# Top-k attention into a cosine-gated MLP: small VectorE steps between MAX8, the P@V scale on GpSimd, the weight shift and weight loads moved

## The chip, the cores and the metric

The kernel runs on one core of a Trainium2 chip. The metric is the device time of one execution in microseconds. The abbreviations are those of the profile: PE is TensorE's matmul, PEld its weight load, DVE is VectorE, ACT is ScalarE, POOL is GpSimd, SP is SyncE, which here only issues DMAs. "L475" is line 475 of the kernel before.

## The reference

Everything is float32 in meaning; the two weight matrices arrive as 64-bit floats.

```python
# q, k, v: (8, 8, 576, 64); w_in: (512, 2048); w_out: (2048, 512)
scores = matmul(q, k.T) / sqrt(64)
kth = partition(scores, -32)[..., -32:-31]          # the 32nd largest of each row
scores = where(scores >= kth, scores, -1e9) - max
attn = exp(scores) / (sum(exp(scores)) + 1e-9)
x = matmul(attn, v)  -> (4608 tokens, 512)           # heads side by side
h = x @ w_in
out = (h * cos(h)) @ w_out                           # (4608, 512)
```

## The kernel before, in words

**Units and slots.** Attention is cut into 144 units of 128 tokens and two heads. A unit's scores are a tile of 128 x 2 x 576. The main loop has 145 slots. In slot i the code works on several units at once: it searches the top 32 of unit `u` = i, finishes the softmax of `w` = i - 1, sends `x` = i - 2 through DRAM to be transposed, and, in even slots only, multiplies the pair `z` = (i - 4, i - 3) with V. Slots 0 to 8 are `early_slot`, 9 to 140 are `slot`, 141 to 144 `last_slot`. The schedule is manual: each engine runs its instructions in the order in which the Python code emits them.

**Search (VectorE).** `fold_high` (L244) takes the larger of each two scores into `rest` (288 wide), and GpSimd makes the smaller ones in `low` by an integer sum and difference (`fold_sum` L262, `fold_low` L271). `topk_round` then runs MAX8 (L342) and MATCH_REPLACE8 (L345) on the two heads: three rounds with replacement and a fourth without on `rest`, then two on `low`. `low` and `rest` have one buffer each, so `fold_sum` of a unit waits for the last search on `low` of the unit before. Between two units' searches stand small steps: `merge_first` (L330) and `merge_second` (L335) find the 32nd value of `w`, `bounds` (L354, L359) makes its negative and the exponent's bias, and `reciprocal` (L385, L386) adds up the softmax sums of `x` and inverts them.

**Softmax (ScalarE).** `mask` (L366, L368) and `exponentials` (L376). `take_scores` (L233, L234) copies the scores of the next unit out of PSUM.

**The way of P to the matmul.** `send(x)`: GpSimd's `split` (L403, L405) writes the float words as 16-bit halves, with the reciprocal appended; SP writes them to DRAM (`write_halves`, L413), waits for the landing, and issues a transposing DMA (`transposes`, L419) into `pT`. Two slots later at most, PE's `values` (L456) multiplies with V into the PSUM tile `rim`, ACT's `take_values` (L463) copies the result of two units to `xT`, and `scale_values` (L475, on VectorE) multiplies `xT` by the transposed reciprocal.

**MLP.** Per block of 128 tokens: `ff1` (L521) on PE, `take_first` on ACT (L535, L537), then on GpSimd the range reduction `reduce_first` (L557) and `reduce_second` (L566), the sine on ACT (`sines`, L576), the product on GpSimd (`gate`, L583), `ff2` (L596) on PE, and the output (L606). `feed(n)` emits up to n of these matmul pieces at fixed places of a slot; how many is a matter of a credit counter and of counters of finished steps, all in Python, so the order is fixed when the program is built.

**Order of a slot before.** `reciprocal(x)`; `topk_first` (merges of `w`, folds of `u`, `bounds(w)`, round 0); `decode_second`; `send(x)`; `fold_low`; rounds 1 to 3; then `feed(1)`; from slot 28 on `values(z)` and then the scores of the next units (before slot 28 the scores come first); the ACT steps; `scale_values(z)`; weight loads and the loads of q, k, v; `gate(1)`; `feed`; the range reduction; `feed`. In the steady part GpSimd's order is: in even slots `fold_sum`, `split`, `fold_low`, `reduce_first`, `reduce_second`; in odd slots `fold_sum`, `split`, `fold_low`, `gate`.

**Weights.** 32 chunks are loaded as 64-bit words into a ring of seven buffers, shared with the MLP's `g` tiles (`load_weights`, L115), and turned into float32 by ACT (`decode_first`, L128), GpSimd and VectorE (`decode_second`, L138 and the shift L141) and GpSimd (`decode_third`, L151). This ends in slot 13.

Of the kernel before, what the change touches and what calls it, by code (L numbers as in the profile page):

```python
# [10 lines left out]
F32 = mybir.dt.float32  # L11
# [4 lines left out]
ALU = mybir.AluOpType  # L16

P = 128
TOPK = 32
# [11 lines left out]
def kernel(  # L31
# [9 lines left out]
    nc = tc.nc  # L41
    ctx.enter_context(tc.manual_schedule())
    B, H, D, S = qT.shape
    DM, DF = moe_w_in.shape
    NT = S // P
# [4 lines left out]
    HS = S // 2  # L50
# [7 lines left out]
    small = ctx.enter_context(tc.tile_pool(name="small", bufs=4))  # L58
# [25 lines left out]
    for i in range(DF // CW):  # L84
        w = consts.tile([P, NC, CW], F32, tag=f"w_in{i}", name=f"w_in{i}")
# [47 lines left out]
    def decode_second(n):  # L133

        for _ in range(min(n, len(wq["second"]))):
            st, w = wq["second"].popleft()
            wi, lo = w.bitcast(I32), st[:, :, 0]
            nc.gpsimd.tensor_scalar(  # L138
                out=lo, in0=lo.bitcast(U32), scalar1=2.0**-29, scalar2=1.0, op0=ALU.mult, op1=ALU.mult
            )  # L140
            nc.vector.tensor_scalar(  # L141
                out=wi, in0=wi, scalar1=3, scalar2=None, op0=ALU.logical_shift_left
            )
            wq["third"].append((st, w))
# [121 lines left out]
    def fold_low(u):  # L266

        if not u["folds"]:
            return
        low = u["low"].bitcast(I32)  # L270
        nc.gpsimd.tensor_tensor(  # L271
            out=low, in0=low, in1=u["rest"][:, :, HS:S].bitcast(I32), op=ALU.subtract
        )
# [15 lines left out]
    def topk_first(u, w):  # L289

        u["top"] = tops[u["n"] % len(tops)]
        merges = w and w["folds"]
        if merges:
            merge_first(w)
        if u["folds"]:
            if u["n"] > EARLY:
                fold_sum(u)
            fold_high(u)
        else:
            u["rest"] = work.tile([P, 2, S], F32, tag="rest", name="rest", bufs=1)  # L300
        if merges:
            merge_second(w)
        if w:
            bounds(w)
        if u["folds"] and u["n"] <= EARLY:
            fold_now(u)
        topk_round(u, 0)

    def topk_round(u, rnd):
        top, rest, lasts = u["top"], u["rest"], TOPK // 8 - 1  # L310
        end = TOPK - 1 - 8 * rnd
        at = top[:, :, end : end - 8 if rnd < lasts else None : -1, 0]
        if u["folds"]:
            search(at, rest[:, :, HS:S] if rnd == 0 else rest[:, :, 0:HS], rest[:, :, 0:HS], rnd < lasts)
        else:
            search(at, u["s"] if rnd == 0 else rest, rest, rnd < lasts)
        if rnd < lasts:
            return
        del u["rest"]
        if u["folds"]:  # L320
            low = u.pop("low")
            for k in range(TOPK // 16):
                search(top[:, :, 1 + 8 * k : 9 + 8 * k, 1], low, low, k < TOPK // 16 - 1)

# [10 lines left out]
            op=ALU.max,  # L337
        )

    def search(to, src, rest, more):  # L340
        for j in range(2):
            nc.vector.max(to[:, j], src[:, j])  # L342
        if more:
            for j in range(2):
                nc.vector.match_replace(rest[:, j], to[:, j], src[:, j], NEG)  # L345

    def bounds(u):

        top = u.pop("top").rearrange("p j r i -> p j (r i)")
        end = 2 * TOPK  # L350
        if not u["folds"]:
            nc.vector.tensor_copy(out=top[:, :, end - 1], in_=top[:, :, 0])
        u["less"] = top[:, :, end : end + 2]
        nc.vector.tensor_reduce(  # L354
            out=u["less"], in_=top[:, :, end - 2 : end].unsqueeze(3), axis=mybir.AxisListType.X,
            op=ALU.max, negate=True,
        )
        u["nd"] = small.tile([P, 2], F32, tag="nd", name="nd")
        nc.vector.tensor_reduce(  # L359
            out=u["nd"], in_=top[:, :, end - 1 : end + 1], axis=mybir.AxisListType.X, op=ALU.add  # L360
        )

    def mask(u):
# [15 lines left out]
            )  # L379


    def reciprocal(u):
        u["rden"] = small.tile([P, 2], F32, tag="rden", name="rden")
        den = small.tile([P, 2], F32, tag="den", name="den")
        nc.vector.tensor_reduce(out=den, in_=u.pop("den"), axis=mybir.AxisListType.X, op=ALU.add)  # L385
        nc.vector.reciprocal(u["rden"], den)  # L386

    def normalise(u):
        s, rden = u["s"], u.pop("rden")
# [81 lines left out]
    def scale_values(us):  # L471

        for u in us:
            to = block_of[u["tok"]]["xT"][:, u["hp"]]
            nc.vector.tensor_tensor(out=to, in0=to, in1=u.pop("pT")[:, 2 * NT + 1], op=ALU.mult)  # L475

    widths = [P] * (B * S // P)
    blocks, block_of = [], {}
# [100 lines left out]
    def gate(n):  # L579
        for _ in range(min(n, len(sined))):  # L580
            blk, g, x = sined.popleft()
            eng = nc.vector if ff["end"] else nc.gpsimd
            eng.tensor_tensor(out=g, in0=g, in1=x, op=ALU.mult)  # L583
            blk["gated"].append(ff["tick"])
# [98 lines left out]
    def early_slot(i, u, w):  # L683
        n = 3 if i < 6 else 2
        topk_first(u, w)
        if i == 0:
            decode_second(1)
        scores(units[i + 1])
        for load, b, hp in at_slot.get(i, []):
            load(b, hp)  # L690
        load_weights(n)
        if w:
            mask(w)
            exponentials(w)
        topk_round(u, 1)

        decode_second(n)
        if w:
            reciprocal(w)
        topk_round(u, 2)  # L700
        topk_round(u, 3)
        if w:
            normalise(w)
        take_banks()
        take_scores(units[i + 1])
        gate(1)
        decode_third()
        feed(2)
        reduce_first()
        reduce_second()  # L710
        if i != NP:
            decode_first(n - 1)
        if w:
            transposes_now(w)
        feed(1)
        decode_first(n - len(wq["second"]))
        if w:
            values([w])
            take_values([w])
        feed(2)  # L720
        sines(2)
# [5 lines left out]
        transposes(x)  # L727

    def slot(i, u, w, x, z):
        if x:  # L730
            reciprocal(x)
        if u:
            topk_first(u, w)
            decode_second(2)
        if x:
            send(x)
        if u:
            fold_low(u)
            topk_round(u, 1)
            topk_round(u, 2)  # L740
            topk_round(u, 3)
        made = scored.get(i, [])
        if z:
            take_banks()
        feed(1)

        ahead = i < EARLY + 5 * NP
        if z and not ahead:
            values(z)
        for m in made:  # L750
            scores(m)
        if z and ahead:
            values(z)


        late = len(made) > 0

        decoding = i < EARLY + 8
        if i % 2 and not decoding:
            sines(1)  # L760
        if w:
            mask(w)
        take_banks()
        if w and late:
            exponentials(w)
        if z and not ahead:
            take_values(z)
        take_scores(units[i + 1])
        if z and ahead:
            take_values(z)  # L770
        if z:
            scale_values(z)
        if w and not late:
            exponentials(w)
        load_weights(2)
        for load, b, hp in at_slot.get(i, []):
            load(b, hp)
        gate(1)
        feed(1 if len(made) == 2 else 2)
        take_banks()  # L780
        decode_third()
        decode_first(2)
        reduce_first()
        reduce_second()
        feed(1 if len(made) == 2 else 3)
        if decoding or i == LAST:
            sines(1)

    def last_slot(i, u, w, x, z):
        if x:  # L790
            reciprocal(x)
        if u:
            topk_first(u, w)
            fold_low(u)
            topk_round(u, 1)
        if not u:
            bounds(w)
        mask(w)
        exponentials(w)
        take_banks()  # L800
        sines(1)
        if z:
            values(z)
        if i + 1 < NU:
            scores(units[i + 1])
        if z:
            take_values(z)
            scale_values(z)
        if i + 1 < NU:
            take_scores(units[i + 1])  # L810
        if x:
            send(x)
        reciprocal(w)
        normalise(w)
        if u:
            topk_round(u, 2)
            topk_round(u, 3)
        gate(2)
        feed(2)
        transposes_now(w)  # L820
        take_banks()
        reduce_first()
        reduce_second()
        feed(1)
        values([w])
        take_values([w])
        feed(2)
# [71 lines left out]
```

## Time and profile before

| what | value |
|---|---|
| median of 3 runs | 1504.34 us (1501.29 to 1507.36) |
| the profiled execution | 1504.25 us |
| its span | 1502.3 us |
| PE, PEld busy | 1414.7, 1015.1 us |
| DVE, ACT, POOL busy | 1392.8, 1096.0, 1162.0 us |
| mean granted TensorE clock | 0.966 |
| slots 28 to 139 (starts of L330) | 312.4 to 1387.2 us |

The span is the time from the first to the last instruction that the profile holds; the execution is 1.95 us longer. Busy time is the union of the instructions' intervals; since matmuls are pipelined and their ends are modelled, busy PE is not the same as PE at its peak. Small shapes are written partitions x elements. The lines below `## 5` of the page give for each group the count, the busy time, the mean duration of one in ns, and the idle time of the engine just before them with what ended it.

### The profile page before, as it was taken

To read this page: it belongs to the slowest core of one execution; us is meant where nothing else is said; L and a number is where in the kernel's file an instruction comes from. 1 tells how busy PE (TensorE), PEld (TensorE's weight loads), DVE (VectorE), ACT (ScalarE), POOL (GpSimd) and SP (SyncE) were. 2 spreads that over 40 slices of the span, in tenths; PEclk is the share of its full clock that TensorE was granted. 3 is DMA by queue.
4 is the path that set the end of the run, shared out by engine and by line. 5 is a ranking of instruction groups with operands and counts; after the bars stand their busy time and mean duration, and the time that the engine had idled before them with its cause. 6 is when DMAs were issued, how large, how long until landed. Compare 5 with 4: busy or idle time off the path is not lost.

```text
span 1502.3 us, 30590 instructions
## 1 busy us (share of the span) xinstructions
PE 1414.7 (94%) x10360; PEld 1015.1 (68%) x10360; DVE 1392.8 (93%) x5209; ACT 1096.0 (73%) x1974; POOL 1162.0 (77%) x836
## 2 busy tenths in 40 slices
PE   4778599999999999999999999999999999999899
PEld 3566267776777667777767767677677776777675
DVE  7998899999999999999989999999999998999931
ACT  4665667777777777777777777777777786777551
POOL 4678877888888888888878888888888887888510
PEclk6689799999999999999999999999999999999999
DMA  8423475556655566556655566645765556555200
GB/s 276 147 97 107 139 200 150 164 148 186 168 161 146 148 194 181 163 148 180 177 164 146 144 176 179 173 138 168 196 173 143 147 163 162 164 149 148 78 8 14
DMA packets 405549, 229.54 MB, mean 153 GB/s; under 512 B 355088, under 2 KB 371728, under 8 KB 405392
## 3 DMA queue, kind: packets, MB, share of 16 engines
q1 hardware_dynamic: 399984, 217.93, 52.5%
q10 hardware_dynamic: 5408, 9.65, 1.7%
q8 instruction: 82, 1.34, 0.4%
q14 instruction: 75, 0.61, 0.1%
HBM read 45.09 MB, written 95.94 MB: 94 GB/s over the span
## 4 chain that ended last, share of the span: by engine, by line
DVE 63%; PE 22%; ACT 6%; DMA 5%; issue 2%; POOL 1%; SPq 1%; POOLq 0%; DVEq 0%; ACTq 0%
DVE top L342 28%; DVE rest L345 17%; PE mm L521 9%; PE o L596 8%; DVE low L345 6%; DVE rest L244 5%; PE rim L456 3%; DMA pT<-rows 3%; PE sc L223 2%; DVE xT L475 2%; ACT s L376 1%; DVE top L354 1%; DVE top L330 1%; DVE nd L359 1%; DMA v<-in_v_dram 1%
## 5 line engine op out<-in xcount | busy, mean ns | idle before, releaser
L521 PEld LDWEIGHTS mm<-xT,w_in 128*128 128x128 f32 x4608 | 539.0, 192 | 77.1 <-issue 65.3
L596 PE MATMUL o<-w_out,g 128*128 128x512 f32 x1152 | 541.8, 604 | 19.1 <-POOL w_out L151 15.9
L521 PE MATMUL mm<-xT,w_in 128*128 128x128 f32 x4608 | 544.4, 276 | 7.3 <-DVE xT L475 3.9
L342 DVE MAX8 top<-rest 128x8 f32<-128x288 f32 x1148 | 469.9, 451 | 0.0
L345 DVE MATCH_REPLACE8 rest<-top,rest 128x288 f32<-128x288 f32 (+1 forms) x860 | 376.9, 445 | 0.0
L262 POOL TENSOR_TENSOR low<-s 128x576 int32<-128x576 int32 x133 | 192.6, 1448 | 198.5 <-DVE den L385 119.3
L596 PEld LDWEIGHTS o<-w_out,g 128*128 128x128 f32 x1152 | 203.8, 192 | 207.6 <-issue 181.4
L403 POOL COPY halves<-s 128x2304 uint16<-128x2304 uint16 x132 | 278.1, 2107 | 0.2
L376 ACT ACTIVATE s<-s,nd 128x576 f32<-128x576 f32 x288 | 220.6, 768 | 14.0 <-ACT ob L606 13.2
L342 DVE MAX8 top<-low 128x8 f32<-128x288 f32 x568 | 229.2, 446 | 0.0
L368 ACT ACTIVATE s<-s,top 128x576 f32<-128x576 f32 x288 | 206.1, 766 | 0.0
L535 ACT ACTIVATE g<-mm 128x512 f32<-128x512 f32 x144 | 85.9, 596 | 159.7 <-PE mm L521 155.1
L271 POOL TENSOR_TENSOR low<-low,rest 128x576 int32<-128x576 int32 x133 | 188.3, 1416 | 0.6 <-DVE top L335 0.5
L456 PE MATMUL rim<-pT,v 128*64 128x128 f32 (+1 forms) x2560 | 164.2, 273 | 19.4 <-DMA pT<-rows 10.5
L456 PEld LDWEIGHTS rim<-pT,v 128*64 128x64 f32 x2560 | 134.8, 141 | 70.0 <-ACT nd L366 22.0
L223 PE MATMUL sc<-k,q 64*128 64x448 f32 (+1 forms) x640 | 157.1, 592 | 10.7 <-DMA k<-in_k_dram 10.2
L566 POOL TENSOR_TENSOR x<-g,x 128x1024 f32<-128x1024 f32 x68 | 160.7, 2363 | 5.7
L583 POOL TENSOR_TENSOR g<-g,x 128x1024 f32<-128x1024 f32 x68 | 160.7, 2363 | 3.7 <-ACT x L576 3.7
L233 ACT COPY s<-sc 128x896 f32<-128x896 f32 x144 | 130.4, 906 | 4.2 <-PE sc L223 4.2
L345 DVE MATCH_REPLACE8 low<-top,low 128x288 f32<-128x288 f32 x284 | 123.6, 443 | 0.0
L463 ACT COPY xT<-rim 128x256 f32<-128x256 f32 (+1 forms) x78 | 27.8, 357 | 128.0 <-PE rim L223 104.2
L244 DVE TENSOR_TENSOR rest<-sc,s 128x576 f32<-128x576 f32 x142 | 106.3, 748 | 8.2 <-ACT s L234 8.2
(59 smaller groups left out, 1387.4 us busy)
## 6 DMA issues: line engine op xcount, KB each, us to landing
rows<-halves SPq DMA_DIRECT2D x132, 640.0 KB, 3.1
out_dram<-ob ACTq DMA_DIRECT2D x36, 256.0 KB, 3.0
q<-in_q_dram SPq DMA_DIRECT2D x31, 288.0 KB, 3.4
st<-in_moe_w_in_dram SPq DMA_DIRECT2D x16, 512.0 KB, 5.6
v<-in_v_dram SPq DMA_DIRECT2D x32, 256.0 KB, 3.1
st<-in_moe_w_out_dram SPq DMA_DIRECT2D x16, 512.0 KB, 3.9
k<-in_k_dram SPq DMA_DIRECT2D x31, 144.0 KB, 3.6
k<-in_k_dram SPq DMA_DIRECT2D x32, 128.0 KB, 3.5
```

Source lines behind the costliest of these rows:

```text
L223: nc.tensor.matmul(to[r0 : r0 + rows, j, 0 : k1 - k0], st["q"][d, q0 : q0 + rows], st["k"][d, k0:k1], start=True, stop=True,)
L244: nc.vector.tensor_tensor(out=u["rest"][:, :, HS:S], in0=sc[:, :, 0:HS], in1=s[:, :, HS:S], op=ALU.max)
L262: nc.gpsimd.tensor_tensor(out=u["low"].bitcast(I32), in0=s[:, :, 0:HS], in1=s[:, :, HS:S], op=ALU.add)
L271: nc.gpsimd.tensor_tensor(out=low, in0=low, in1=u["rest"][:, :, HS:S].bitcast(I32), op=ALU.subtract)
L342: nc.vector.max(to[:, j], src[:, j])
L345: nc.vector.match_replace(rest[:, j], to[:, j], src[:, j], NEG)
L368: nc.scalar.activation(out=s[:, j], in_=s[:, j], func=AF.Prelu, bias=less[:, j, 1:2], scale=1.0, alpha=FAR)
L376: nc.scalar.activation(out=s[:, j], in_=s[:, j], func=AF.Exp, bias=nd[:, j : j + 1], scale=SCALE, accum_out=den[:, j, 0:1],)
L403: nc.gpsimd.tensor_copy(out=halves[:, :, 0 : 2 * S], in_=s.rearrange("p (k h) -> p h k", h=2))
L456: nc.tensor.matmul(o[d, to], lhsT, rhs, start=c == 0, stop=c == NT)
L521: nc.tensor.matmul(mm[:, at : at + w], w_in[f // FC][:, c, (f % FC) * P : (f % FC + 1) * P], blk["xT"][:, c], start=c == 0, stop=c == NC - 1,)
L596: nc.tensor.matmul(o, g[:, at : at + P], w_out[f], start=f == 0, stop=f == NF - 1)
```

## The change

- `search` takes a list `between`: after the MAX8 of each of the two heads one small step is put. In round 0 these are the two steps of `bounds(w)`, now `bounds` and `distances`; in the last search of a unit (the second one on `low`) they are the two steps of `reciprocal`, now `sums` and `reciprocal`, of the unit `w` of that slot. Before, `bounds` stood ahead of round 0 and `reciprocal` at the start of the next slot.
- `scale_values` is a GpSimd instruction, and is emitted after `gate(1)` and ahead of the range reduction.
- `decode_second` is emitted just ahead of round 3, which with its searches on `low` is moved behind `exponentials`.
- `load_weights` is the first step of a slot.
- In `last_slot` rounds 2 and 3 come before `normalise`.

```diff
@@ topk_first / topk_round / search @@
-        if w:
-            bounds(w)
...
-        topk_round(u, 0)
+        topk_round(u, 0, [lambda: bounds(w), lambda: distances(w)] if w else ())
...
-    def search(to, src, rest, more):
+    def search(to, src, rest, more, between=()):
         for j in range(2):
             nc.vector.max(to[:, j], src[:, j])
+            if between:
+                between[j]()
         if more:
             for j in range(2):
                 nc.vector.match_replace(rest[:, j], to[:, j], src[:, j], NEG)
@@ reciprocal @@
+    def sums(u):
+        den = small.tile([P, 2], F32, tag="den", name="den")
+        nc.vector.tensor_reduce(out=den, in_=u["den"], axis=mybir.AxisListType.X, op=ALU.add)
+        u["den"] = den
+
     def reciprocal(u):
         u["rden"] = small.tile([P, 2], F32, tag="rden", name="rden")
...
+        nc.vector.reciprocal(u["rden"], u.pop("den"))
+
+    def both(u):
+        return [lambda: sums(u), lambda: reciprocal(u)] if u else ()
@@ scale_values @@
-            nc.vector.tensor_tensor(out=to, in0=to, in1=u.pop("pT")[:, 2 * NT + 1], op=ALU.mult)
+            nc.gpsimd.tensor_tensor(out=to, in0=to, in1=u.pop("pT")[:, 2 * NT + 1], op=ALU.mult)
@@ early_slot @@
-        if w:
-            reciprocal(w)
-        topk_round(u, 2)
+        topk_round(u, 2, both(w))
         topk_round(u, 3)
@@ slot @@
-        if x:
-            reciprocal(x)
-        if u:
-            topk_first(u, w)
-            decode_second(2)
+        load_weights(2)
+        topk_first(u, w)
         if x:
             send(x)
-        if u:
-            fold_low(u)
-            topk_round(u, 1)
-            topk_round(u, 2)
-            topk_round(u, 3)
+        fold_low(u)
+        topk_round(u, 1)
+        topk_round(u, 2)
...
-        if z:
-            scale_values(z)
         if w and not late:
             exponentials(w)
-        load_weights(2)
+        decode_second(2)
+        topk_round(u, 3, both(w))
         for load, b, hp in at_slot.get(i, []):
             load(b, hp)
         gate(1)
+        if z:
+            scale_values(z)
         feed(1 if len(made) == 2 else 2)
@@ last_slot @@
-        reciprocal(w)
+        if u:
+            topk_round(u, 2, both(w))
+            topk_round(u, 3)
+        else:
+            sums(w)
+            reciprocal(w)
         normalise(w)
-        if u:
-            topk_round(u, 2)
-            topk_round(u, 3)
```

More of the change, by code (lines that the diff above doesn't have):

```diff
@@ L302, in topk_first, with topk_round @@
             merge_second(w)
-        if w:
-            bounds(w)
         if u["folds"] and u["n"] <= EARLY:
             fold_now(u)
-        topk_round(u, 0)
-    def topk_round(u, rnd):
+        topk_round(u, 0, [lambda: bounds(w), lambda: distances(w)] if w else ())
+    def topk_round(u, rnd, between=()):
         top, rest, lasts = u["top"], u["rest"], TOPK // 8 - 1
@@ L313, in topk_round @@
         if u["folds"]:
-            search(at, rest[:, :, HS:S] if rnd == 0 else rest[:, :, 0:HS], rest[:, :, 0:HS], rnd < lasts)
+            search(
+                at, rest[:, :, HS:S] if rnd == 0 else rest[:, :, 0:HS], rest[:, :, 0:HS], rnd < lasts,
+                between if rnd < lasts else (),
+            )
         else:
-            search(at, u["s"] if rnd == 0 else rest, rest, rnd < lasts)
+            search(at, u["s"] if rnd == 0 else rest, rest, rnd < lasts, between)
         if rnd < lasts:
@@ L322, in topk_round @@
             for k in range(TOPK // 16):
-                search(top[:, :, 1 + 8 * k : 9 + 8 * k, 1], low, low, k < TOPK // 16 - 1)
+                more = k < TOPK // 16 - 1
+                search(
+                    top[:, :, 1 + 8 * k : 9 + 8 * k, 1], low, low, more,
+                    () if more or rnd < lasts else between,
+                )
     def merge_first(u):
@@ L352, in bounds, with distances @@
             nc.vector.tensor_copy(out=top[:, :, end - 1], in_=top[:, :, 0])
-        u["less"] = top[:, :, end : end + 2]
+        less = u["less"] = top[:, :, end : end + 2]
+        u["near"] = top[:, :, end - 1 : end + 1]
         nc.vector.tensor_reduce(
-            out=u["less"], in_=top[:, :, end - 2 : end].unsqueeze(3), axis=mybir.AxisListType.X,
+            out=less, in_=top[:, :, end - 2 : end].unsqueeze(3), axis=mybir.AxisListType.X,
             op=ALU.max, negate=True,
         )
+    def distances(u):
         u["nd"] = small.tile([P, 2], F32, tag="nd", name="nd")
         nc.vector.tensor_reduce(
-            out=u["nd"], in_=top[:, :, end - 1 : end + 1], axis=mybir.AxisListType.X, op=ALU.add
+            out=u["nd"], in_=u.pop("near"), axis=mybir.AxisListType.X, op=ALU.add
         )
@@ L379, in exponentials @@
             )
+    def sums(u):
+        den = small.tile([P, 2], F32, tag="den", name="den")
+        nc.vector.tensor_reduce(out=den, in_=u["den"], axis=mybir.AxisListType.X, op=ALU.add)
+        u["den"] = den
     def reciprocal(u):
         u["rden"] = small.tile([P, 2], F32, tag="rden", name="rden")
-        den = small.tile([P, 2], F32, tag="den", name="den")
-        nc.vector.tensor_reduce(out=den, in_=u.pop("den"), axis=mybir.AxisListType.X, op=ALU.add)
-        nc.vector.reciprocal(u["rden"], den)
+        nc.vector.reciprocal(u["rden"], u.pop("den"))
+    def both(u):
+        return [lambda: sums(u), lambda: reciprocal(u)] if u else ()
     def normalise(u):
@@ L789, in last_slot @@
     def last_slot(i, u, w, x, z):
-        if x:
-            reciprocal(x)
         if u:
@@ L795, in last_slot @@
             topk_round(u, 1)
-        if not u:
+        else:
             bounds(w)
+            distances(w)
         mask(w)
@@ L812, in last_slot @@
             send(x)
-        reciprocal(w)
+        if u:
+            topk_round(u, 2, both(w))
+            topk_round(u, 3)
+        else:
+            sums(w)
+            reciprocal(w)
         normalise(w)
-        if u:
-            topk_round(u, 2)
-            topk_round(u, 3)
         gate(2)
```

## The prediction, made before the changed kernel ran

> **What bounds the kernel now.** I read the page first, then the table of engines by stretches of 50 us, the groups of VectorE, the waits, and the timelines of GpSimd, ACT, SP and PE over slots 66 to 69. The page and one row of the stretches (columns: us, then busy us of PE, PEld, DVE, ACT, POOL, the granted clock, DMA share, GB/s):
>
> ```profile
> PE 1414.7 (94%) x10360; PEld 1015.1 (68%) x10360; DVE 1392.8 (93%) x5209; ACT 1096.0 (73%) x1974; POOL 1162.0 (77%) x836
> 600.00:650.00 50.00, 50.00 (x410) 36.02 (x409) 49.48 (x192) 40.37 (x73) 43.67 (x31) 1.00 0.55 155
> ```
>
> In the steady part VectorE and PE are both full, and GpSimd has 6.3 us in 50 left. The starts of L330 put a number on it: even slots take 9.67 us, odd ones 9.27, a pair 18.94, nearly everywhere from slot 28 (312.4 us) to slot 140 (1387.2 us). PE is hardly slower: from pair to pair L463, which follows PE's work of the slot, starts up to 0.17 us earlier in its slot (7.7, 7.5, 7.2, 7.0 in slots 60 to 66), so PE's work in a pair is about 18.77 us. A lighter VectorE alone can win 0.17 us a pair.
>
> Now the timeline of GpSimd over slots 66 (even) to 68 (start, us, engine, line):
>
> ```profile
> 677.66 1.43 POOL L271 TENSOR_TENSOR low<-low,rest 128x576 int32<-128x576 int32 x1
> 679.04 1.06 POOL L557 TENSOR_SCALAR x<-x 128x1024 f32<-128x1024 int32 x1
> 680.18 2.37 POOL L566 TENSOR_TENSOR x<-g,x 128x1024 f32<-128x1024 f32 x1
> 683.14 1.53 POOL L262 TENSOR_TENSOR low<-s 128x576 int32<-128x576 int32 x1 [0.59 <-DVE top L342]
> 684.61 2.11 POOL L403 COPY halves<-s 128x2304 uint16<-128x2304 uint16 x1
> 686.65 0.41 POOL L405 COPY halves<-rden 128x256 uint16<-128x256 uint16 x1
> 687.02 1.41 POOL L271 TENSOR_TENSOR low<-low,rest 128x576 int32<-128x576 int32 x1
> 688.38 2.36 POOL L583 TENSOR_TENSOR g<-g,x 128x1024 f32<-128x1024 f32 x1
> 692.84 1.41 POOL L262 TENSOR_TENSOR low<-s 128x576 int32<-128x576 int32 x1 [2.09 <-DVE den L385]
> ```
>
> The same stretch on ACT (its copies of P@V), SP and PE, from their timelines:
>
> ```profile
> 680.88 0.37 ACT L463 COPY xT<-rim 128x256 f32<-128x256 f32 x1 [1.08 <-PE rim L223]
> ...
> 687.09 0.34 SPq L413 DMA_DIRECT2D rows<-halves  x1
> 690.35 2.73 SPq L419 DMA_TRANSPOSE pT<-rows  x1
> ...
> 696.43 1.04 PE L456 MATMUL rim<-pT,v 128*64 128x128 f32 x16
> 697.62 1.02 PE L223 MATMUL sc<-k,q 64*128 64x448 f32 x4
> 699.89 0.37 ACT L463 COPY xT<-rim 128x256 f32<-128x256 f32 x1 [2.10 <-PE rim L223]
> ```
>
> GpSimd starts a slot with L262 when VectorE has let go of `low`, and runs without a pause. In the even slot the range reduction starts at 679.04, while L463 ends only at 681.25. That copy waits not for P@V but for the scores behind it on PE, in 57 of its waits (waits: us in total, times, longest; then the DMA's median us to landing):
>
> ```profile
> ACT xT L463 <- PE rim L223: 104.2, 57, 5.6
> SPq L419 <- DMA rows<-halves: 354.5, 119, 5.0
> pT<-rows SPq DMA_TRANSPOSE x132, 4.9
> ```
>
> **VectorE's part.** From the last MAX8 of one unit to the first of the next the starts in an odd slot step by 0.172 (L385), 0.082 (L386), 0.120 (L330), 0.664 (L244), 0.214 (L335), 0.193 (L354), 0.075 us (L359): 1.52 us. L385, L335 and L354 are each followed by an instruction that needs their result; L359 is not, and costs 0.075. Put between MAX8 of other data, I take every small step at 0.07 to 0.08, and L335 at 0.12 because round 0 still waits for the fold: 0.07 + 0.08 + 0.12 + 0.66 + 0.12 + 0.14 = 1.19. That is 0.33 us a slot. The scale leaves too: its two instructions step 0.190 and 0.202. So VectorE's pair falls by 0.66 + 0.39 = 1.05 to 17.9 us.
>
> [...]
>
> **GpSimd's part.** No row shows a float product of 128x128 on GpSimd. Its cost is taken from two-input rows: 1.29 us for 512 elements (L151), 2.363 for 1024 (L566), so 2.1 ns an element and 0.22 fixed, 0.49 for one and 0.95 for two. The bounds are 0.8, twice L405's 0.40, and 2.6, twice L151. I take the line's value: both rows have its kind of operands, and only the size lies outside.
>
> The Trainium skill (GPSIMD Engine Reference, "Engine selection") sends a two-input elementwise step to VectorE, as GpSimd is about twice as slow. By that ratio and L475's mean of 325 ns the two would be 1.3 us, and the sum 0.35 x 56 = 20 us higher (an estimate).
>
> **The wait.** This decides. The scale is emitted ahead of the range reduction, and it needs L463. In slot 66 GpSimd is free at 679.04 but L463 ends at 681.25: 2.2 us in which L557 and L566, and behind them the next slot's L262, `split` and L271, are queued. On GpSimd the even slot's leavings would end at 681.25 + 0.05 + 0.95 + 1.14 + 2.30 = 685.7 rather than at 682.5; the next L262 starts 2.5 us late or more, and VectorE, whose search on `low` has 1.9 us of slack behind L271 (which ends at 688.4, the search begins 6.72 into the slot, at 690.3), is stopped. The sine, first on ACT in the odd slot, waits for L566 too, and behind it `mask` and the exponentials, on which `sums`, now in the middle of the last search, waits.
>
> It also closes a ring, as the odd slot's `split` now follows L463 of the even slot, and the next even slot's L463 follows that `split` by DRAM:
> - scale 0.05 + 0.95 = 1.00;
> - L557 1.14, L566 2.30, L262 1.40, L403 2.04, L405 0.41 = 7.29 (starts above);
> - write issue 0.03; write, landing, transpose, landing: 3.26 + 4.9 = 8.16 in slot 67. Over all odd slots the trace gives 7.8 to 10.1, median 8.16, mean 8.54. I take 8.3: q and k loads stand less in its way;
> - P@V of the second unit 0.05 + 1.19, scores 2.22, L463 0.42 = 3.88.
>
> Sum 20.5 us a pair, against 18.94 typical and 1074.8 / 56 = 19.19 on average with all interruptions. The ring binds in slots 28 to 139, where P@V is ahead of the scores: 56 x 20.5 - 1074.8 = **+73 us**. With the shortest legs (7.8, scale 0.8) it is 19.85, +37; with the DMA legs at their upper quartile, 9.3, it is 21.5, +129; with the scale at 2.6 it is 22.15, +166. Neither upper end is likely for the mean over 56 pairs, and they go to rival 3. VectorE's 17.9 and PE's 18.77 fit inside, so what they save is waited away. Before slot 28 the scores come ahead of P@V; the ring is then 2.2 less, 18.3, and PE remains: about -1 us.
>
> **Weights.** In slots 9 to 13 loads come up to a slot earlier, and none is left after slot 11 by the planner's counters. Before, slots 12 and 13 took 29 us together because the last chunks came late (ACT L128 waited 15.4 us for DMA, PE L596 15.9 us for L151). I take -10 us, between -20 and +8: SP may stand on a full ring ahead of the halves' write (its waits at L115 for POOL reached 10.4 us). The shift itself (L141, 0.42 to 0.66 us, 32 times, most in the early slots) is the same work.
>
> **Edges.** Eight early slots with 0.25 saved: -2. Last slots: +1. Sum: 1504.25 + 73 - 1 - 10 - 2 + 1 = **1565 us**. The profiled execution is 0.1 us from the median of the three runs, so this stands against 1504.34.
>
> **Rivals.**
> 1. *The scale fits into GpSimd's pauses* (faster). GpSimd idles 2.1 + 0.6 us a pair, and needs 0.95. For it: busy times alone allow it. It decides where L463 ends within 1.75 us of L271's end, before about 6.9 us into the even slot; the trace has it at 6.4 in slots 88, 124 and 140 but at 7.3 to 8.6 elsewhere. Then PE's 18.77 bounds: 56 x -0.17, -14 of interruptions halved, -12 of the rest: 1504 - 10 - 7 - 12 = 1475 us. Chance 0.09.
> 2. *GpSimd's own round without the DMA leg*: P@V is ready in time, and only the queue shifts. A round is then L463's end (7.4 into the slot) + 0.95 + 3.45 + 5.25 + 2.4 = 19.4: +0.46 from the typical pair, +26, with -12: 1518 us. Chance 0.11. Against it: the transposed P landed only some 2 us into the even slot before.
> 3. *The ring with a dear scale or slow DMA legs* and weights that gain nothing: 21.3 to 22.15 a pair, +118 to +166, less 2: 1620 to 1668 us. Chance 0.08.
> 4. *Gains and waits cancel*: 1497 to 1511 us, 0.04.
>
> The forecast has 0.68, with pairs from 20.0 (+45) to 21.0 (+101) and the weights' bounds: 1527 to 1605. I give 1520 to 1605 us, which leaves out rivals 1 and 3, rival 4 and part of 2. A measurement of this kernel can tell about 0.5% (7.5 us) from no change. Faster is rival 1, 0.09; the same is rival 4 and the low end of rival 2, 0.06; slower is the rest, 0.85.
>
> **What would show it.** Right: pairs of 20 to 21 us; L475 on POOL some 0.49 us each, with a wait for ACT L463 of 2 to 4 us ahead of it; L566 ending after the next slot's VectorE start; PE waiting for `pT` in most even slots; VectorE waiting for POOL L271 or for the exponentials; small steps 0.07 apart on VectorE. Wrong: GpSimd not waiting for L463, or pairs below 18.9.

## The result, and the profile after

The changed kernel takes 1657.51 us (median of 4 runs, 1654.57 to 1660.95) against 1505.21 us (4 runs) for the kernel before on the same chip: a ratio of 1.1016, 95% interval 1.0981 to 1.105. The forecast had the direction and the mechanism, but its time, 1565 us, was 93 us too low, and its range ended at 1605. The profiled execution took 1655.45 us, with a span of 1653.6 us; the numbers below are from it.

From the page after: busy engines, the chain that ended last, the groups of the scale and of the search on `low`, and the output's DMA (us to landing at the end).

```profile
PE 1466.0 (89%) x10360; PEld 1037.1 (63%) x10360; DVE 1350.6 (82%) x5077; ACT 1090.4 (66%) x1974; POOL 1210.7 (73%) x968
...
PE 44%; DMA 25%; ACT 10%; POOL 7%; DVE 7%; issue 6%; SPq 2%; ACTq 0%; POOLq 0%
...
L347 DVE MAX8 top<-low 128x8 f32<-128x288 f32 x568 | 240.5, 450 | 112.8 <-POOL low L271 112.8
...
L491 POOL TENSOR_TENSOR xT<-xT,pT 128x128 f32<-128x128 f32 x132 | 57.7, 459 | 259.4 <-ACT xT L479 259.3
...
out_dram<-ob ACTq DMA_DIRECT2D x36, 256.0 KB, 4.3
```

No engine is full any more. VectorE has fallen from 93% to 82% of the span, and a quarter of the chain is DMA. The scale is cheap, 459 ns each, but GpSimd stood idle for 259 us in front of it. The waits (us in total, times, longest) show who handed the wait on to whom:

```profile
POOL xT L491 <- ACT xT L479: 259.3, 64, 12.8
ACT xT L479 <- PE rim L223: 217.9, 58, 6.6
...
ACT x L592 <- POOL x L582: 134.1, 62, 3.2
DVE top L347 <- POOL low L271: 112.8, 65, 3.3
...
PE rim L472 <- DMA pT<-rows: 103.5, 59, 3.6
```

Read backwards this is a circle. GpSimd waits for ACT's copy of P@V, the copy for PE's scores behind P@V, and P@V for the transposed P, whose `split` stands in GpSimd's queue behind the scale. VectorE and the sine (L592) wait for what is late on GpSimd. One turn of the circle, from GpSimd's timeline (start, us, engine, line):

```profile
778.17 0.88 POOL L491 TENSOR_TENSOR xT<-xT,pT 128x128 f32<-128x128 f32 x2 [5.92 <-ACT xT L479]
779.01 1.05 POOL L573 TENSOR_SCALAR x<-x 128x1024 f32<-128x1024 int32 x1
780.14 2.36 POOL L582 TENSOR_TENSOR x<-g,x 128x1024 f32<-128x1024 f32 x1
782.47 1.41 POOL L262 TENSOR_TENSOR low<-s 128x576 int32<-128x576 int32 x1
783.82 2.11 POOL L419 COPY halves<-s 128x2304 uint16<-128x2304 uint16 x1
785.86 0.41 POOL L421 COPY halves<-rden 128x256 uint16<-128x256 uint16 x1
...
797.96 0.87 POOL L491 TENSOR_TENSOR xT<-xT,pT 128x128 f32<-128x128 f32 x2 [1.89 <-ACT xT L479]
```

SP then writes and transposes, PE multiplies, ACT copies (their timelines):

```profile
786.30 0.34 SPq L429 DMA_DIRECT2D rows<-halves  x1
789.25 2.71 SPq L435 DMA_TRANSPOSE pT<-rows  x1
```

```profile
794.01 1.09 PE L472 MATMUL rim<-pT,v 128*64 128x128 f32 x16 [0.77 <-DMA pT<-rows]
```

```profile
797.51 0.37 ACT L479 COPY xT<-rim 128x256 f32<-128x256 f32 x1 [1.79 <-PE rim L223]
```

From scale to scale it is 797.96 - 778.17 = 19.79 us, and this turn is a quick one. The stretches, from the starts of `merge_first` (L335 now), stand so, in us; the last row is a run of the study, told below:

| | to slot 14 | 14 to 27 | 28 to 139 | from 140 | a pair in 28 to 139, mean, median |
|---|---|---|---|---|---|
| before | 174.5 | 137.9 | 1074.8 | 115.1 | 19.19, 18.94 |
| forecast | 162.5 | 136.9 | 1148 | 116.1 | 20.5 |
| after | 164.1 | 149.7 | 1223.9 | 115.9 | 21.85, 21.46 |
| e12 | 174.0 | 148.9 | 1162.7 | 114.5 | 20.76, 20.28 |

The weights gained their 10 us and the ends are as forecast; slots 28 to 139 lost 149 us where 73 had been expected, and slots 14 to 27 lost 12 where 1 was to be gained. The mean legs of the ring, over 55 pairs, show which of its terms were wrong (e5 and e7 are runs of the study, too):

| leg, us | forecast | after | e5 | e7 | e12 |
|---|---|---|---|---|---|
| copy's end to scale, the two scales | 1.00 | 0.92 | 0.92 | 0.92 | 0.92 |
| L573, L582, L262, split | 7.29 | 7.26 | 7.26 | 7.26 | 7.25 |
| issue of the write | 0.03 | 0.03 | 0.03 | 0.03 | 0.03 |
| write to transpose's landing | 8.3 | 9.05 | 8.83 | 8.32 | 8.39 |
| landing to end of the copy | 3.88 | 4.58 | 4.07 | 4.36 | 4.19 |
| sum | 20.5 | 21.84 | 21.11 | 20.89 | 20.78 |

GpSimd's 8.3 us were right to a tenth. The excess is 0.75 in the DMA leg and 0.70 in the leg of P@V. Two sights in the trace name a suspect for each.

**PE at half clock.** Where PE waited long between the P@V of the two units, many of the matmuls behind the wait take twice the time. PE's timeline, the second unit of slot 70, to be held against 1.09 us for the same sixteen at 794.01 above:

```profile
772.58 1.81 PE L472 MATMUL rim<-pT,v 128*64 128x128 f32 x16 [2.40 <-DMA pT<-rows]
```

The stretches (columns: us, then PE, PEld, DVE, ACT, POOL busy, granted clock, DMA share, GB/s) around this wait, and around one of 2.30 us in slot 58 that did no harm:

```profile
769.39:772.80 3.41, 1.01 (x20) 0.77 (x16) 3.41 (x14) 2.51 (x6) 2.86 (x3) 1.00 1.21 296
772.80:776.21 3.41, 3.41 (x24) 2.46 (x22) 3.36 (x14) 0.00 (x0) 0.00 (x0) 0.50 0.42 123
776.21:779.62 3.41, 3.41 (x20) 1.86 (x17) 0.41 (x1) 1.88 (x4) 1.45 (x3) 1.00 1.12 270
...
646.50:649.91 3.41, 2.02 (x44) 1.74 (x46) 3.41 (x13) 0.74 (x2) 1.09 (x1) 1.00 0.48 195
649.91:653.32 3.41, 3.41 (x20) 1.82 (x17) 1.95 (x9) 1.84 (x4) 1.41 (x3) 1.00 0.89 192
```

The granted clock is 0.50 from 772.80 to 776.21, through most of P@V and the first scores, and the copy ends 1.6 us later. Of 22 pairs with 2.1 us or more between the starts of two successive P@V matmuls, 20 took over 4.3 us from P@V to the copy; of the other 33, 3 did.

The Trainium skill (TensorE: Matmul & The Clock Gate, "What's actually happening") has the clock fall to half after at least one idle window of about 3.4 us. The half agrees with the 0.50 here, but PE was not idle for 3.4 us: the pause was 2.40 us, and in the 3.41 us up to the fall PE was busy for 1.01 us. In slots 28 to 139 of this run the clock fell 21 times, each time for 3.41 us, and all 21 falls lie on one grid of steps of 3.413 us. In the step ahead of a fall PE was busy for 1.59 us at most; ahead of the 338 other points of the grid at which the clock was full and stayed so, for 1.63 us at least. So the length of a pause alone does not decide: one of 1.92 us (slot 34) brought a fall, the one of 2.30 us above did not.

**The output in the way of the transposing DMA.** In the changed kernel an output (L624, 256 KB) leaves at the end of an odd slot, mostly 10.7 to 15.2 us into it, and is in flight with the odd slot's transposing DMA in 28 of the 56 pairs: these land after 6.23 us on average, the other 28 after 5.31. Before, it left some 4 us into an even slot, and 6 of 56 were met. The cause is the weights' order (e7 below); by the code, with loads a little earlier the counters of `feed` let a piece of the MLP go sooner, and the whole stream of pieces stands elsewhere in the slots from then on.

### The profile page after: what moved, and what is told of

The parts are those of the page before. It is cut to its first block, busy times and chain, and to the rows that moved or that the text cites. A ratio compares the mean times of both kernels' runs of the same rounds, so it can differ in the third digit from the quotient of the medians.

```text
span 1653.6 us, 30494 instructions
## 1 busy us (share of the span) xinstructions
PE 1466.0 (89%) x10360; PEld 1037.1 (63%) x10360; DVE 1350.6 (82%) x5077; ACT 1090.4 (66%) x1974; POOL 1210.7 (73%) x968
## 4 chain that ended last, share of the span: by engine, by line
PE 44%; DMA 25%; ACT 10%; POOL 7%; DVE 7%; issue 6%; SPq 2%; ACTq 0%; POOLq 0%
DMA pT<-rows 17%; PE mm L537 14%; PE o L612 13%; PE sc L223 7%; PE rim L472 7%; DMA rows<-halves 5%; DVE top L347 3%; POOL x L582 2%; ACT s L233 2%; PE rim L223 2%; ACT s L386 2%; POOL low L262 2%; ACT s L378 2%; DVE rest L244 1%; DVE rest L352 1%
## 5 line engine op out<-in xcount | busy, mean ns | idle before, releaser
L347 DVE MAX8 top<-rest 128x8 f32<-128x288 f32 x1148 | 481.4, 454 | 0.0
L347 DVE MAX8 top<-low 128x8 f32<-128x288 f32 x568 | 240.5, 450 | 112.8 <-POOL low L271 112.8
L472 PE MATMUL rim<-pT,v 128*64 128x128 f32 (+1 forms) x2560 | 175.6, 284 | 111.5 <-DMA pT<-rows 103.5
L472 PEld LDWEIGHTS rim<-pT,v 128*64 128x64 f32 x2560 | 139.4, 146 | 172.6 <-DMA pT<-rows 111.2
L491 POOL TENSOR_TENSOR xT<-xT,pT 128x128 f32<-128x128 f32 x132 | 57.7, 459 | 259.4 <-ACT xT L479 259.3
L262 POOL TENSOR_TENSOR low<-s 128x576 int32<-128x576 int32 x133 | 188.0, 1413 | 61.0 <-DVE rden L399 58.2
L223 PE MATMUL sc<-k,q 64*128 64x448 f32 (+1 forms) x640 | 177.4, 655 | 14.2 <-DMA k<-in_k_dram 14.2
L479 ACT COPY xT<-rim 128x256 f32<-128x256 f32 (+1 forms) x78 | 27.8, 357 | 238.1 <-PE rim L223 217.9
L592 ACT ACTIVATE x<-x,halfpi 128x1024 f32<-128x1024 f32 x72 | 82.6, 1149 | 138.2 <-POOL x L582 134.1
L582 POOL TENSOR_TENSOR x<-g,x 128x1024 f32<-128x1024 f32 x68 | 160.6, 2362 | 5.7
```

Of the source, the lines that this page charges most:

```text
L223: nc.tensor.matmul(to[r0 : r0 + rows, j, 0 : k1 - k0], st["q"][d, q0 : q0 + rows], st["k"][d, k0:k1], start=True, stop=True,)
L262: nc.gpsimd.tensor_tensor(out=u["low"].bitcast(I32), in0=s[:, :, 0:HS], in1=s[:, :, HS:S], op=ALU.add)
L472: nc.tensor.matmul(o[d, to], lhsT, rhs, start=c == 0, stop=c == NT)
L582: nc.gpsimd.tensor_tensor(out=x, in0=g, in1=x, op=ALU.subtract)
```

## The experiments

Two theories were set against each other: the ring, through the place of the scale on GpSimd, and a loss by something else in the change (the scale's price, the new VectorE order, the weights). Behind them stood the question what the two excess legs are worth. All ratios are to the kernel before, run beside.

**e1: the scale on VectorE again, at the new place.**

```diff
-            nc.gpsimd.tensor_tensor(out=to, in0=to, in1=u.pop("pT")[:, 2 * NT + 1], op=ALU.mult)
+            nc.vector.tensor_tensor(out=to, in0=to, in1=u.pop("pT")[:, 2 * NT + 1], op=ALU.mult)
```

> The changed kernel with one word undone: the scale of P@V is a VectorE instruction again, behind the last search of its slot; all else stays. Ring theory (GpSimd waits for the copy of P@V, and the split of the odd slot, the transposing DMA, P@V and the scores lead back to that copy): no ring is left, VectorE's pair is 8.99 x 2 + 0.39 = 18.4 us, so PE's 18.8 bounds; 56 x 18.8 = 1053 against 1223.9 now: 1655 - 171 = 1484, between 1475 and 1500 us, and POOL no longer waits for ACT. Rival (the moved rounds, the decode or the loads cost the time, by VectorE standing in its search for the exponentials or SP for its ring): stays above 1600 us.

1502.16 us, ratio 1.0001 (0.9986 to 1.0016), just above the 1475 to 1500 that were expected. All the loss goes with GpSimd's scale. But the rest of the change, which was to make the kernel faster, is worth nothing measurable: the median pair is 18.70 us, 0.24 less than before, while the mean is 19.29. There are more interruptions: 28 of 56 transposing DMAs meet an output and land after 5.81 us, the others after 4.98.

**e2: the kernel before, with only the scale moved to GpSimd and behind `gate(1)`.**

```diff
-            nc.vector.tensor_tensor(out=to, in0=to, in1=u.pop("pT")[:, 2 * NT + 1], op=ALU.mult)
+            nc.gpsimd.tensor_tensor(out=to, in0=to, in1=u.pop("pT")[:, 2 * NT + 1], op=ALU.mult)
...
-        if z:
-            scale_values(z)
         if w and not late:
...
         gate(1)
+        if z:
+            scale_values(z)
```

> The kernel before with one edit alone: the scale is a GpSimd instruction behind gate, ahead of the range reduction. Ring theory: the ring does not contain VectorE, so pairs are again 21 to 22.5 us and the whole 1640 to 1670 us, although VectorE's small steps stand as before. Rival (the new order of VectorE's steps, with sums inside the search, is needed for the loss): well below, 1504 to 1560 us, as only GpSimd's 0.92 us a pair and a queue shift remain.

1599.53 us, ratio 1.0638 (1.0601 to 1.0675): less than was expected of the scale as the whole cause. The scale alone brings a ring of 21.05 us a pair on average, 20.29 in the median (in the profiled execution, which took 1612.11 us, the longest of four), and some 96 us; the other 58 us of the change need its other parts.

**e3: the changed kernel, with the scale on GpSimd behind the range reduction.**

```diff
         gate(1)
-        if z:
-            scale_values(z)
...
         reduce_first()
         reduce_second()
+        if z:
+            scale_values(z)
```

> The changed kernel with the scale still on GpSimd, but emitted behind the range reduction of the slot. Ring theory: the reduction runs in the pause before the copy, the wait for the copy falls to under 1 us, and the next slot's low sum starts at most 1 us late, inside VectorE's slack of 1.9 us: pairs 18.8 to 19.1, 1480 to 1505 us. Rival (a GpSimd product of 128x128 is itself too dear, or slows VectorE by a shared port): still above 1560 us.

1495.98 us, ratio 0.9963 (0.9941 to 0.9986). The same two instructions on the same engine, 3.4 us further back in its queue, and some 160 us are gone. The waits and GpSimd's timeline of this run:

```profile
POOL xT L491 <- ACT xT L479: 34.5, 15, 8.6
...
DVE top L347 <- POOL low L271: 3.3, 3, 1.8
```

```profile
692.66 2.36 POOL L582 TENSOR_TENSOR x<-g,x 128x1024 f32<-128x1024 f32 x1
694.97 0.87 POOL L491 TENSOR_TENSOR xT<-xT,pT 128x128 f32<-128x128 f32 x2
695.80 1.42 POOL L262 TENSOR_TENSOR low<-s 128x576 int32<-128x576 int32 x1
```

At 694.97 the copy has long ended, the scale waits for nothing and fits into GpSimd's pause. The price of the scale was not the trouble; its place was. Slots 14 to 27 take 136.2 us here against 149.7, so the loss there comes from the place too.

**e4: the scores ahead of P@V throughout** (one line).

```diff
-        ahead = i < EARLY + 5 * NP
+        ahead = True
```

> The changed kernel, with the scores ahead of P@V in all slots (in the changed kernel only before slot 28). PE's work is the same, only these two change places. Ring theory: the stretch from P@V's start to the copy's end falls from 4.5 us on average to about 2.1 (P@V 1.25, a score copy 0.4, the copy 0.4), so pairs fall from 21.86 to about 19.5 and the whole to about 1525 us (1500 to 1560). Rival (only the queue behind GpSimd's wait counts, not the way back through PE): no change, 1640 to 1665 us.

1546.7 us, from one run only. It takes the 2.2 us of scores out of the ring, and a pair falls from 21.85 to 20.03, a little less than was expected. GpSimd still waits 152.8 us for L479: the ring is cut shorter, not open.

**e5: six transposes that compute nothing needed, on PE between the P@V of the two units**, so that PE does not stand idle there.

```diff
         for i, u in enumerate(us):
+            if i == 1:
+                for _ in range(6):
+                    nc.tensor.transpose(room[1][:, 0:P], ident, ident)
             pT = u["pT"]
```

> The changed kernel with six more 128x128 transposes on PE (some 1.3 us at full clock) in the pause between P@V of a pair's first and second unit; their result is used by nobody. Clock theory: after a pause of over some 2.4 us PE runs at half its clock, and P@V and scores take 5.5 instead of 3.9 us; with the pause filled to below that, the 22 or so slow pairs become fast: -1.6 x 22 = -36 us, and the shortest pauses (1.0 us) cost at most 0.3 us each: 1615 to 1635 us, copy's stretch 3.9 in nearly all pairs. Rival (the slow P@V comes from memory traffic at that time): the stretch stays at two values and the time does not fall, 1650 to 1675 us.

1613.01 us, ratio 1.0755 (1.0732 to 1.0778): 44 us less by giving PE more to do. The mean clock is 0.973 instead of 0.953, the leg from landing to copy 4.07 instead of 4.58. Of 19 pairs whose successive P@V starts are 2.1 us or more apart only 2 are above 4.3 us. In slots 28 to 139 the clock falls 2 times instead of 21. So the pause cost through the clock. Not all of the 44 us is the clock's: 0.51 us a pair, some 29 us, went from the leg of P@V, and 0.22 us, some 12 us, from the DMA leg.

**e6: the output's DMA with 16 of its 128 rows**; the other rows of the output are left unwritten.

```diff
-                nc.scalar.dma_start(out=out[row : row + P, :], in_=ob)
+                nc.scalar.dma_start(out=out[row : row + 16, :], in_=ob[0:16])
```

> The changed kernel, but each output tile is written for 16 of its 128 rows only (32 KB instead of 256 KB); the rest of the output is left out. Collision theory: in the changed kernel the output leaves at the end of odd slots and meets the transposing DMA of the odd slot in about half the pairs, which then lands in 6.36 instead of 5.32 us; without it -1.0 x 27 = -27 us, and, as shorter pauses keep the clock up, up to 20 more: 1605 to 1635 us. Rival (the next slot's write of the halves, 640 KB, is what delays the transposing DMA): 1650 us or more.

1608.55 us, ratio 1.0728 (1.07 to 1.0756), 49 us less; the odd transposing DMA lands after 5.28 us on average, instead of 5.79. The output's bytes do disturb it. The whole DMA leg is 8.56 us here, so they stand for 0.49 of the 0.75 us of its excess.

**e7: the changed kernel with `load_weights` and `decode_second` where they were.**

```diff
-        load_weights(2)
         topk_first(u, w)
+        decode_second(2)
...
-        decode_second(2)
         topk_round(u, 3, both(w))
+        load_weights(2)
```

> The changed kernel with weight loads and decode_second put back where they were before; the scale stays on GpSimd ahead of the range reduction and the small steps between MAX8. Phase theory: the new order of the weights shifts the stream of MLP pieces by one, so that the output leaves at the end of odd slots; with the old order it leaves 3 to 4 us into even slots as before, the transposing DMA is undisturbed, and the ring has 20.3 to 21 us a pair: 1590 to 1615 us, near the kernel before with the scale alone moved (1599.5). Rival (the small steps between MAX8 make the ring longer, by bringing the even slot's write of halves earlier): 1640 to 1665 us.

1605.89 us, ratio 1.0702 (1.0667 to 1.0737), 52 us less, and inside what was expected. The outputs leave 3.9 us into even slots again, 10 of 56 transposing DMAs are met by one, and the landing takes 5.08 us; with that the DMA leg is the forecast's. This is the other part that e2 lacked. It costs the start its 10 us: slot 14 begins at 174.1 us, not at 164.1.

**e8 and e9: e3 and e1, each with the weights' order of before.** The edit is that of e7.

> Scale on GpSimd behind the range reduction, small steps between MAX8, weight loads and decode_second as before. Phase theory: against the same with the new weight order (1496.0) the transposing DMA is undisturbed, so most pairs keep PE's 18.7 us: about 20 us less in the steady part, about 12 us lost in the early slots: 1475 to 1495 us. Rival (interruptions come from the q and k loads alone): 1500 to 1512 us, as the early slots' gain is lost and nothing comes back.

> Scale on VectorE, small steps between MAX8, weight loads and decode_second as before: of the change only VectorE's new order is left. Phase theory: against the same with the new weight order (1502.2) the output leaves in even slots again and the steady part loses its interruptions: pairs 18.7 with few longer ones, 1485 to 1498 us. Rival (the phase matters only inside the ring): 1505 to 1512 us, as the early gain of the new weight order is lost.

1489.25 us, ratio 0.9931 (0.9915 to 0.9948), and 1496.11 us, ratio 0.9959 (0.9934 to 0.9984), both as expected. Without the ring too, the new order of the weights loses some 16 us later, in the profiled executions, for the 9 to 13 us that it gains at the start.

**e10: e3 with one piece of the MLP less at one place of slot 14**, which moves the outputs while the weights stay early.

```diff
-        feed(1 if len(made) == 2 else 2)
+        feed((1 if len(made) == 2 else 2) - (i == 14))
```

> Scale on GpSimd behind the range reduction, small steps between MAX8, new order of weights, and one MLP piece less in the middle feed of slot 14, which moves the stream of pieces back by one: the output leaves in even slots, though the weights are loaded first. Phase theory: the early gain of the new weight order (7 us at slot 28) and the undisturbed steady part together: 1478 to 1488 us, below both 1496.0 (new order, output in odd slots) and 1489.3 (old order). Rival (the weight order itself, not the phase, made the difference): 1492 to 1500 us.

1481.38 us, ratio 0.9858 (0.9836 to 0.9881): 1.4% faster than the kernel before. The outputs leave 0.9 us into even slots and still meet 28 of the 56 transposing DMAs, but these land after 5.41 us, where it was 6.05 in e3; the early gain is kept (slot 14 at 163.4 us), and the pair is 19.07 us on average, against 19.33 in e3.

**e11: the same edit on the changed kernel itself.**

> The changed kernel with only that one piece less in slot 14. Phase theory: the ring stays, the output no longer meets the odd slot's transposing DMA: about 20.9 us a pair and 1590 to 1612 us, as with the old weight order (1605.9). Rival (weight order itself): 1645 to 1665 us.

1648.94 us, ratio 1.0984 (1.0949 to 1.1018): a miss. The outputs moved as planned, to 0.5 us into even slots, but in the ring the odd transposing DMA is still in flight then: 28 of 56 are met, landing after 6.27 us against 5.07. What counts is the overlap in time, not which slot the output leaves in. And the shift put a piece of `ff1` in PE's queue ahead of P@V, as the waits of this run show:

```profile
PE mm L537 <- ACT x L553: 113.9, 59, 2.5
...
PE rim L472 <- DMA pT<-rows: 15.1, 17, 1.9
```

PE now stands at that piece, for ACT, instead of at P@V, for the DMA. P@V is late all the same; from the landing to the copy it is 4.75 us on average.

**e12: e7's and e5's edits together**, so that both excess legs are shortened and the ring is left.

> The weights' order of before (as in the run that put it back alone) together with the six idle transposes between the two units' P@V: both of the terms that the forecast lacked are taken away at once, the ring is left. If the ring's forecast legs are right apart from these two terms, a pair takes 20.3 to 20.6 us on average, the transposing DMA lands after 4.9 to 5.2 us, the copy ends 3.9 to 4.0 us after P@V begins, and the time is 1575 to 1595 us, within 30 of the forecast's 1565. The rival: a further term is hidden (another wait of PE or ACT in the ring), and the two do not add up: about 1605 us, as with either alone, pairs of 20.9 or more.

1602.78 us, ratio 1.0674 (1.062 to 1.0728), near the rival's time, though the ring is nearly the forecast's: 20.28 us in the median and 20.76 on average, legs in the table above. The stretches tell why: slots 28 to 139 take 1162.7 us, 15 more than forecast, and the two stretches ahead of them 12 and 12 more, one since the weights' gain is given up with their order, the other by the loss in slots 14 to 27. The two edits do not add up (44 and 51 us in slots 28 to 139 each alone, 61 together). One reason is that a transposed P that lands earlier also spares PE long pauses: in e7, where only the DMA was relieved, 16 pairs instead of 22 had P@V starts 2.1 us or more apart, and the leg of P@V fell from 4.58 to 4.36 as well. What is left over the forecast in e12 is 0.31 us in the leg of P@V, which was not taken further.

## Why the prediction was wrong in its size

**Right.** The ring is what happened. Its GpSimd part was 8.21 us against 8.32, its scale 459 ns each against 0.49. VectorE's saving was right as well. Its timeline after (start, us):

```profile
791.69 0.46 DVE L347 MAX8 top<-rest 128x8 f32<-128x288 f32 x1
792.07 0.14 DVE L362 TENSOR_REDUCE top<-top 128x4 f32<-128x4 f32 x1
792.13 0.45 DVE L347 MAX8 top<-rest 128x8 f32<-128x288 f32 x1
792.50 0.14 DVE L369 TENSOR_REDUCE nd<-top 128x2 f32<-128x4 f32 x1
792.55 0.08 DVE L352 MATCH_VALUE_LOAD rest<-top,rest 128x8 f32 x1
```

A small step between MAX8 of other data costs 0.06 us (792.07 to 792.13; 792.50 to 792.55), forecast 0.07. An undisturbed slot is 9.0 us, against 9.67 and 9.27 before, and the ring waits it away, as was said. The weights brought the forecast 10 us by slot 14.

**The first step that failed** is the DMA leg of the sum: 8.3 us was taken, with "q and k loads stand less in its way", though the trace of before had 8.54 on average, and it measured 9.05. In slots 28 to 139 that is 56 x 0.75 = 42 us. The landing of the transposing DMA had been taken from a trace in which hardly any output crossed it. The working costed the weights' move by its own loads and shifts and never asked where `feed` would put the outputs afterwards. e6 shows the output's bytes as the cause of 0.49 of the 0.75 us; with the old order of the weights, which also puts every other piece back in its place, the leg is 8.32 (e7) and 8.39 (e12).

**The second** is "P@V of the second unit 0.05 + 1.19, scores 2.22, L463 0.42 = 3.88", which measured 4.58: 56 x 0.70 = 39 us. It was taken from a PE at full clock that hardly stood still, and the forecast itself had PE wait in most pairs. In 20 of 55 pairs a long wait halves the clock of just the matmuls that the ring waits for. e5 shows it. With the -6 us of the other legs these two make 75 of the 76 us missed here.

**The third** is "-1 us" before slot 28. With the scores ahead of P@V the pair was to stay at PE's 18.8; from slot 20 on it was 19.2 to 20.4, and slot 19 took 21.7 us, with a wait of GpSimd for L479 of up to 12.8 us. Together 12 us, and e3 shows that the scale's place is the cause. The trace has the legs. The P@V of slot 18 came late, as the scores ahead of it on PE waited 3.19 us for a load of k (0.63 us before) and the clock fell at 213.01 us while they ran; slot 19 then waited for it through GpSimd. From slot 22 on the write of the halves landed after 4.9 to 5.2 us instead of some 3.0, so that the DMA leg was 9.8 to 10.1 us and not 8.3; what held the write up is not shown.

Two numbers of the working were off without weight for this. The starts of L463 that it lists (7.7, 7.5, 7.2, 7.0) fall by 0.24 us a pair, not 0.17, so PE's pair was 18.70 us, as the medians of e1 and e3 are. And the upper bounds of its terms add up to 1504.25 + 101 - 1 + 8 - 2 + 1 = 1611, not 1605; the measured time lies outside both.

The rivals: the first, that the scale fits into GpSimd's pauses, is true only behind the range reduction (e3, e10), and its 1475 us is near e10's 1481. The second, a round without the DMA leg, is refuted by PE's 59 waits for `pT`, 103.5 us in all, and the fourth by the time. The third had the size (21.3 to 22.15 a pair, 1620 to 1668 us) but only a part of its reason: slow DMA legs, yes, but the scale was not dear, the weights did gain their 10 us, and the clock was not in it; that its time fits is in part luck.

## What to carry to other kernels

Before an instruction is put on an engine with an in-order queue, ask what stands behind it and whether its own input depends, by way of other engines and DRAM, on that: here 0.9 us of work closed a ring and cost some 160 us, and 3.4 us further back in the queue it cost nothing. When a ring binds, its legs are not those of the trace before: PE's new pauses can slow its clock, and transfers meet others, so they are priced from pairs in which that happens. And a change that shifts when a planner emits its pieces moves every transfer that hangs on them; look where they leave before and after.

## What the runs showed of the hardware

- PE's granted clock fell to 0.50 for 3.41 us at a time, on a fixed grid of 3.413 us steps, when PE had been busy for less than some 1.6 us of the step before. Over slots 28 to 139 of all fourteen kernels 83 of 85 falls had at most 1.59 us of work ahead of them (the other two 1.71, in the kernel before, and 2.16, in e7), and after no step with less than 1.52 us did the full clock stay. Six transposes in the pause, whose result nobody uses, brought the falls from 21 to 2 (e5).
- A 256 KB write to DRAM on ACT's queue, in flight with a transposing DMA from SP's, went with a landing of the latter after 6.23 instead of 5.31 us (changed kernel) and 6.27 instead of 5.07 us (e11); with an eighth of the bytes it was 5.42 against 5.14 us (e6).
- A VectorE step of 0.14 us between MAX8 of other data delays the next by 0.06 us; before, followed by an instruction that needs its result, it took 0.17 to 0.21 us.
